# Regrouping batch 0 and batch 1 of a Nystrom attention, gated FFN and soft-MoE kernel: slot tables, paired G products, low bits on ScalarE, three Tanh

## The chip, the cores and the metric

The kernel runs on one core of one Trainium2 chip. The metric is the device time of one execution in microseconds; the median of three runs before the change is 675.02 us (674.23 to 676.28).

## The reference

Three stages follow one another on 8 batches of 576 tokens with 8 heads of 64 (512 features):

```python
q_lm, k_lm = segment means of q, k over 18 tokens       # 32 landmarks per head
A, Bm, C = softmax(q k_lm'), softmax(q_lm k_lm'), softmax(q_lm k')
Z = Bm' / (norm1(Bm) * norminf(Bm));  6 times: Z = 2 Z - Z Bm Z
x = A Z C v                                             # attention, as 4608 x 512
x = (silu(x @ w_gate) * (x @ w_val)) @ w_out            # d_ff = 1536
logits = x @ phi                                        # 32 slots: 8 experts x 4
d = softmax of logits over all 4608 tokens;  c = softmax over the 32 slots
out = c @ expert_ffn(d' x)                              # 8 experts, 512 -> 1024 -> 512
```

## The kernel before

**The loop.** After `first_attention` (attention of batch 0), the main loop runs over batches `b` 0 to 7 and, in each, over twelve chunks `j` of 128 hidden features. `unit(b, j, slot)` does one chunk: for each half of the tokens (288 columns) six matmuls into a PSUM tile `pg` (`mm3`, line 945), an activation on ScalarE (Silu, or Tanh with a multiplication more on VectorE), six matmuls into `pv`, and a product `hT = u * pv` on VectorE (lines 972, 974). There are 288 matmuls of `mm3` in a batch. The weights of these matmuls are `G`, the product of the attention's `WB` with `w_gate` and `w_val` (`g_product`, line 748): ScalarE casts it to `GH` (line 765), VectorE subtracts to get `GL` (`g_low`, line 779). Where `paired(b, j)` holds, one call makes the G of two chunks (512 columns instead of 256).

**The slots.** After each of the four groups of six matmuls `unit` calls `slot(i)`, so that a batch has 48 slots `n = 4 j + i`. Everything else is hung into these slots by the tables in `SCHED`: `u0` (batch 0) and `u` (others) say in which slot of a chunk the next G product, the logits (line 794) and the transposes (line 799) of the chunk before are written; `g_low` follows one slot after the G product. `at1`, `at2`, `at3` list the slots in which the 34 steps of the attention of batch 1, 2 and 3 to 7 are written, one batch ahead: numbers 0 to 7 the landmark sums (line 333), 8 to 11 the scores of A (`m_a`, line 541) and their transposes, 12 to 15 the scores of C (`m_c`) and their copies to `CE` (line 577), 16 to 19 the maxima and exponentials, 22 to 24 the transposes of `CE` (`m_t`, line 631), 26 the product with v, 27 to 32 the six Newton steps (`m_n`, line 672), 33 the new `WB`. Negative numbers are slots of the batch before. `am1` to `am3` do the same for the 17 steps of the softmax of A. `sm1` (batch 1) and `sm` list the ten steps of `softmoe(b - 1)`: copies of the logits, maxima, exponentials (fourth), the transposed exponentials `DN` (fifth, line 867), the spreading of `DN` over partitions (sixth: by twelve DMAs, line 879, and in batch 7 by eight matmuls `m_dr`, line 882), the product `m_d` (seventh, line 913, 144 matmuls), and its addition to `Sacc` (line 923).

**PSUM.** `g`, `m_t`, `m_n`, `m_dr`, and three of the four tiles of `m_a`, `m_c` and `m_d` share the three buffers of the tag `x`; a G product takes two of them until its `GL` is done.

**Batch 0 alone** also converts `w_gate`, `w_val` and `w_out` from 64-bit words (tables `w` and `o`: `f32_top` on ScalarE, line 176, then `f32_bits` on VectorE, lines 192 and 193) and folds `w_out` with phi into `P_sb` (table `p`: `m_wt`, `m_p`, `m_ps`, lines 269, 278, 284).

**What sets the order.** Each engine runs its instructions in the order in which they were issued. From batch 1 on TensorE keeps the order of the program text (`keep_order(mybir.EngineType.PE, middle, ...)`, line 1136, where `middle` is the beginning of batch 1). The order of TensorE in batch 0, and of the other engines throughout, is set by the framework's scheduler, to which the place in the text is a priority. Activations of different tables are fenced by `in_order`. Within a slot the steps run in the order in which the generators were put into `todo`:

```python
    for a in range(1, nb):
        att, asm = attention(a), a_softmax(a)
        for gen, nm in ((att, "at"), (asm, "am")):
            for r in S_[nm + str(min(a, 3))]:
                todo[48 * (a - 1) + r].append(gen)
        sm = softmoe(a - 1)
        for r in S_["sm1" if a == 1 else "sm"]:
            todo[48 * a + r].append(sm)
```

In a slot of batch a the soft-MoE step of batch a - 1 (put in by pass a) thus comes before the attention step of batch a + 1 (put in by pass a + 1).

Of the kernel before, what the change touches and what calls it, by code (L numbers as in the profile page):

```python
# [22 lines left out]
NJ = DFF // 128  # L23
# [31 lines left out]
def nystrom_softmoe_kernel(  # L55
# [681 lines left out]
    def paired(b, j):  # L737
        return 0 < b < nb - 1 and not (b == nb - 2 and j >= NJ - 2)
# [209 lines left out]
    def unit(b, j, slot):  # L948
# [3 lines left out]
        for half in range(2):  # L952
# [3 lines left out]
            by_tanh = 0 < b < nb - 1 and (j, half) in TANH[b > 1]  # L956
# [24 lines left out]
    TANH = [{(5, 0), (5, 1), (6, 0)}, {(1, 1), (2, 0), (2, 1)}]  # L981
# [105 lines left out]
    for a in range(1, nb):  # L1087
        att, asm = attention(a), a_softmax(a)
        for gen, nm in ((att, "at"), (asm, "am")):
            for r in S_[nm + str(min(a, 3))]:  # L1090
                todo[48 * (a - 1) + r].append(gen)
        sm = softmoe(a - 1)
        for r in S_["sm1" if a == 1 else "sm"]:
            todo[48 * a + r].append(sm)
    prev = None
    n_ins = lambda: len(nc.cur_bb.bb.instructions)
    for b in range(nb):
        if b == 1:
            middle = n_ins()
        for j in range(NJ):  # L1100
            p = prev
            def slot(i):
# [27 lines left out]
                if n == (46 if b == 0 else 45) and b + 1 < nb:  # L1130
                    g_unit(b + 1, 0)
                if n == (47 if b == 0 else 46):
                    g_low()
# [211 lines left out]
```

## Time and profile before

| what | value |
|---|---|
| median of the runs | 675.02 us |
| the profiled execution: its time, its span | 674.4 us, 672.6 us |
| busy: TensorE matmul, weight load | 623.9 us (93%), 465.8 us (69%) |
| busy: VectorE, ScalarE, GpSimd | 478.0 us (71%), 298.8 us (44%), 73.3 us (11%) |
| HBM read, written | 91.24 MB, 12.58 MB |

PE is TensorE's matmuls, PEld its weight loads, DVE VectorE, ACT ScalarE, POOL GpSimd, SP SyncE, whose queue (SPq) issues the DMAs. Matmuls are pipelined, and their recorded durations overlap: a busy PE is not PE at its peak. PEclk is the granted share of TensorE's 2.4 GHz. A stretch of this kernel has its own limits, so the batches are read one by one: the first matmul of line 945 starts at 40.4 us, and every 288 of them are a batch, which gives the limits 40.4, 125.9, 200.3, 266.2, 332.1, 398.0, 463.9, 527.7 and 589.8 us for the beginnings of batches 0 to 7 and the end of the last one. Ahead of them lies the attention of batch 0, behind them the expert FFN and the output.

### The profile page before, as it was taken

Reading aid. Unit: us, or ns where it says so; the run is one execution under the profiler, and the core shown is the slowest. Engines: PE = TensorE matmul, PEld = TensorE weight load, DVE = VectorE, ACT = ScalarE, POOL = GpSimd, SP = SyncE. Lnnn points to the kernel's source line nnn. Section 1 sums busy time; section 2 is a strip of 40 time slices with the busy share of each in tenths; the row PEclk is TensorE's granted clock in tenths of the full one; section 3 lists DMA queues with packets and bytes.
Section 4 is the critical chain, followed back from the end, with each engine's and each line's share of the span. In section 5 each row is a group of like instructions: output and inputs, shape, how many; then the busy total and the mean of one; then the engine's idle time right before and its main releaser. Section 6 shows DMA issues by size and latency. Waiting matters only on the chain. (4 is left out here: it accounts for less than half of the span.)

```text
span 672.6 us, 18315 instructions
## 1 busy us (share of the span) xinstructions
PE 623.9 (93%) x7591; PEld 465.8 (69%) x7591; DVE 478.0 (71%) x1154; ACT 298.8 (44%) x764; POOL 73.3 (11%) x81
## 2 busy tenths in 40 slices
PE   5699999998999999999999999999999999989991
PEld 2575667784877877787787778777778777843560
DVE  4999989878578777868785978597856645550441
ACT  2566875445438323732383338233823442320441
POOL 0400012013011101110111012001300000010000
PEclk9799999998999999999999999999999999999996
DMA  8788773233222222222222222122120595699999
GB/s 281 271 322 331 269 280 129 87 113 116 73 72 83 75 72 73 84 75 73 72 86 73 71 87 76 69 71 72 57 86 2 160 378 184 220 288 348 348 369 337
DMA packets 63299, 106.47 MB, mean 158 GB/s; under 512 B 4977, under 2 KB 33009, under 8 KB 61681
## 3 DMA queue, kind: packets, MB, share of 16 engines
q1 hardware_dynamic: 63216, 105.32, 47.1%
q8 instruction: 59, 0.97, 0.6%
q14 instruction: 24, 0.19, 0.1%
HBM read 91.24 MB, written 12.58 MB: 154 GB/s over the span
## 5 line engine op out<-in xcount | busy, mean ns | idle before, releaser
L312 ACT ACTIVATE u<-pg 128x288 f32<-128x288 f32 x174 | 71.9, 413 | 138.4 <-PE pg L945 130.8
L974 DVE TENSOR_TENSOR hT<-u,pv 128x288 f32<-128x288 f32 x174 | 77.7, 447 | 40.1 <-PE pv L945 36.3
L945 PE MATMUL pg<-EH,GH 128*128 128x288 f32 x384 | 93.9, 324 | 2.6 <-ACT GH L765 1.6
L779 DVE TENSOR_TENSOR GL<-g,GH 128x512 fp32r<-128x512 f32 (+1 forms) x122 | 66.4, 572 | 37.7 <-ACT GH L765 37.6
L945 PE MATMUL pg<-EH,GL 128*128 128x288 f32 x384 | 85.7, 299 | 1.7 <-DVE GL L779 1.5
L945 PE MATMUL pv<-EH,GH 128*128 128x288 f32 x384 | 84.0, 298 | 0.0
L945 PE MATMUL pg<-EL,GH 128*128 128x288 f32 x384 | 83.5, 296 | 0.0
L945 PE MATMUL pv<-EL,GH 128*128 128x288 f32 x384 | 82.6, 296 | 0.0
L945 PE MATMUL pv<-EH,GL 128*128 128x288 f32 x384 | 82.2, 295 | 0.0
L765 ACT CAST GH<-g 128x512 fp32r<-128x512 f32 (+1 forms) x122 | 54.2, 495 | 55.0 <-PE g L748 54.9
L945 PEld LDWEIGHTS pg<-EH,GH 128*128 128x128 f32 x384 | 60.0, 189 | 22.8 <-issue 15.5
L799 DVE STREAM_TRANSPOSE HB<-hT 128x576 f32<-128x576 f32 x96 | 74.3, 774 | 1.8
L945 PEld LDWEIGHTS pg<-EH,GL 128*128 128x128 f32 x384 | 62.2, 188 | 4.7 <-DVE GL L779 3.8
L945 PEld LDWEIGHTS pv<-EH,GH 128*128 128x128 f32 x384 | 61.6, 188 | 2.6 <-issue 1.2
L945 PEld LDWEIGHTS pg<-EL,GH 128*128 128x128 f32 x384 | 61.8, 188 | 0.9 <-issue 0.9
L945 PEld LDWEIGHTS pv<-EL,GH 128*128 128x128 f32 x384 | 61.5, 188 | 0.9 <-issue 0.9
L945 PEld LDWEIGHTS pv<-EH,GL 128*128 128x128 f32 x384 | 61.6, 188 | 0.5 <-issue 0.5
L748 PE MATMUL g<-w,WB 64*32 64x512 f32 (+1 forms) x976 | 56.4, 510 | 0.4 <-ACT WB L535 0.4
L794 PE MATMUL l<-hT,P_sb 128*32 128x160 f32 (+1 forms) x768 | 45.2, 298 | 0.8 <-DVE hT L974 0.6
L794 PEld LDWEIGHTS l<-hT,P_sb 128*32 128x32 f32 x768 | 15.2, 108 | 39.8 <-DVE hT L974 16.5
L913 PE MATMUL m_d<-HB,HB 32*32 32x384 f32 x864 | 38.4, 514 | 2.6 <-DMA HB<-DN 2.3
L913 PE MATMUL m_d<-HB,DN 32*32 32x384 f32 x288 | 37.7, 514 | 0.0
(248 smaller groups left out, 946.4 us busy)
## 6 DMA issues: line engine op xcount, KB each, us to landing
k<-in_kT_dram SPq DMA_DIRECT2D x52, 288.0 KB, 3.7
ffn<-in_w_dram SPq DMA_DIRECT2D x13, 1024.0 KB, 9.0
ffn<-in_w_dram SPq DMA_DIRECT2D x24, 512.0 KB, 9.0
HB<-in_w_cat_dram SPq DMA_DIRECT2D x8, 1024.0 KB, 8.0
v<-in_v_dram SPq DMA_DIRECT2D x8, 1024.0 KB, 5.8
q<-in_qT_dram SPq DMA_DIRECT2D x28, 288.0 KB, 3.0
HB<-in_w_out_dram SPq DMA_DIRECT2D x12, 512.0 KB, 5.8
wr<-in_w_cat_dram SPq DMA_DIRECT2D x4, 1024.0 KB, 8.7
```

Source lines behind the costliest of these rows:

```text
L312: i = act.activation(*a, **kw)
L748: pe.matmul(gs[r][32 * hp:32 * hp + 32, 0:256 * n].rearrange("p (u f) -> p u f", u=n), WB[b % 2][64 * r:64 * r + 64, hp, :], w[64 * r:64 * ...
L765: act.copy(H_, g)
L779: dve.tensor_tensor(out=GL, in0=g, in1=GH, op=ALU.subtract)
L794: pe.matmul(L[32 * c:32 * c + 32, 0:32 * k], P_sb[:, j, :], main[:, 0:k, c, :], start=j == 0, stop=j == NJ - 1)
L799: dve.transpose(HB[b % 2][:, S * j:S * j + S].rearrange("p (t r) -> p t r", r=32), hT[:, 0:S].rearrange("p (t r) -> p t r", r=32))
L913: pe.matmul(ms[a][32 * g:32 * g + 32, 0:384].rearrange("p (j f) -> p j f", j=NJ), d_of(a, g, k), hb[32 * a:32 * a + 32, :, 4 * k + g, :], ...
L945: pe.matmul(ps[:, 0:HALF], G_t[b, j, q, sel_][h], e[:, q, ts_], start=n == 0, stop=n == 5)
L974: dve.tensor_tensor(out=o, in0=u, in1=pv[:, 0:HALF], op=ALU.mult)
```

## The change

- **Tables.** All slots of batch 0 change (`w`, `o`, `p`, `at1`, `am1`, `u0`): G, logits and transposes are all written in slot 1 of a chunk, the folding of phi in slots 1 and 3. `at2`, `am2` and `sm1` (attention of batch 2 and soft-MoE of batch 0, both in batch 1) change: `m_a` is written in slot 5 instead of 9, `m_c` in 13 instead of 17, the transposes of `CE` in 17 instead of 23, two slots after the last copy instead of four; the spreading of `DN` in slot 18 instead of 21, `m_d` in slot 25 instead of 24. A new table `sm7` (soft-MoE of batch 6, in batch 7) has `DN` in slot 10 and its spreading in slot 13, where `sm` has both in slot 7.
- **Loads.** `v1` is loaded last of the first loads; `w3` moves ahead of `w4`. The k of batch 2 is loaded in slot 36 (`lq`) instead of 44.
- **Low bits.** For the chunks 2, 3, 5, 7, 9 and 11 of `w`, ScalarE makes the low bits (one activation over 1024 elements) and VectorE one instruction per 512 columns instead of two.
- **G pairs** also in batch 0, from chunk 4 on; the G of batch 1's chunk 0 is written in slot 45 instead of 46.
- **Tanh** in three halves of batch 0; the three of batch 1 move by four slots.
- **The order in a slot.** The soft-MoE steps are put into `todo` in a loop of their own, after all attention steps.

```diff
-    'w': [[-22, 2], [-12, 2], [0, 3], [1, 3], [6, 3], [10, 3], [14, 3], [18, 3], [20, 4], [28, 4], [24, 4], [33, 4]],
-    'o': [[-6, 1], [3, 2], [5, 3], [9, 3], [13, 3], [17, 3], [21, 3], [25, 3], [29, 3], [33, 3], [37, 3], [41, 3]],
-    'p': [[0, 2, 2], [5, 2, 1], [10, 2, 1], [14, 2, 1], [18, 2, 1], [22, 2, 1], [26, 2, 1], [30, 2, 1], [34, 2, 1], [38, 2, 1], [42, 2, 1], [46, 1, 0]],
-    'loads': ['w1', 'q0', 'o0', 'w0', 'v0', 'o1', 'q1', 'v1', 'w2', 'w4', 'p', 'w3'],
-    'at1': [1, 2, 3, 3, 4, 5, 6, 6, 7, 7, 8, 8, 9, 9, 10, 10, 12, 13, 13, 13, 16, 17, 18, 19, 20, 21, 22, 26, 28, 31, 34, 37, 40, 43],
-    'am1': [20, 21, 22, 22, 24, 24, 26, 27, 28, 30, 32, 34, 36, 37, 39, 41, 42],
-    'at2': [-3, -2, -1, 0, 3, 4, 5, 6, 9, 10, 10, 11, 17, 18, 18, 19, 19, 20, 20, 21, 21, 22, 23, 23, 23, 25, 27, 29, 31, 33, 35, 37, 39, 42],
-    'am2': [12, 12, 13, 13, 20, 21, 22, 23, 24, 25, 27, 29, 31, 32, 34, 36, 37],
+    'w': [[-22, 2], [-12, 2], [0, 3], [4, 3], [6, 4], [8, 4], [12, 4], [15, 4], [19, 4], [23, 4], [27, 4], [31, 4]],
+    'o': [[-6, 1], [1, 2], [4, 3], [8, 3], [12, 3], [16, 3], [20, 3], [24, 3], [28, 3], [32, 3], [36, 3], [40, 3]],
+    'p': [[-1, 2, 2], [3, 2, 2], [7, 2, 2], [11, 2, 2], [15, 2, 2], [19, 2, 2], [23, 2, 2], [27, 2, 2], [31, 2, 2], [35, 2, 2], [39, 2, 2], [43, 2, 2]],
+    'loads': ['w1', 'q0', 'o0', 'w0', 'v0', 'o1', 'q1', 'w2', 'w3', 'w4', 'p', 'v1'],
+    'at1': [0, 1, 2, 3, 4, 5, 6, 6, 7, 8, 9, 10, 11, 12, 15, 16, 16, 17, 17, 18, 18, 19, 19, 19, 21, 22, 23, 27, 29, 33, 35, 37, 39, 43],
+    'am1': [11, 12, 13, 13, 18, 18, 20, 22, 23, 24, 25, 28, 30, 31, 32, 33, 36],
+    'at2': [-3, -2, -1, 0, 3, 4, 5, 5, 5, 6, 6, 7, 13, 14, 14, 15, 15, 16, 16, 17, 17, 17, 17, 17, 17, 19, 21, 25, 27, 29, 31, 33, 37, 41],
+    'am2': [7, 8, 8, 9, 16, 17, 18, 19, 19, 20, 22, 23, 25, 26, 27, 28, 30],
     'sm': [1, 2, 3, 6, 7, 7, 25, 26, 26, 28],
-    'sm1': [1, 2, 4, 19, 20, 21, 24, 25, 25, 28],
+    'sm1': [1, 2, 4, 15, 17, 18, 25, 26, 26, 28],
+    'sm7': [1, 2, 3, 6, 10, 13, 25, 26, 26, 28],
-    'u0': [1, 3, 3, 0],
+    'u0': [1, 1, 1, 0],
-    'lw': [0, 0, 0, 0, 0, 0, 0, 0, 0, 0, 0, 0],
+    'lw': [0, 0, 1, 1, 0, 1, 0, 1, 0, 1, 0, 1],
-    'lq': 44,
+    'lq': 36,
...
     def paired(b, j):
-        return 0 < b < nb - 1 and not (b == nb - 2 and j >= NJ - 2)
+        return (b > 0 or j >= 4) and b < nb - 1 and not (b == nb - 2 and j >= NJ - 2)
...
-            by_tanh = 0 < b < nb - 1 and (j, half) in TANH[b > 1]
+            by_tanh = b < nb - 1 and (j, half) in TANH[min(b, 2)]
...
-    TANH = [{(5, 0), (5, 1), (6, 0)}, {(1, 1), (2, 0), (2, 1)}]
+    TANH = [{(4, 1), (5, 0), (5, 1)}, {(4, 0), (4, 1), (5, 0)}, {(1, 1), (2, 0), (2, 1)}]
...
                 todo[48 * (a - 1) + r].append(gen)
+    for a in range(1, nb):
         sm = softmoe(a - 1)
-        for r in S_["sm1" if a == 1 else "sm"]:
+        for r in S_["sm1" if a == 1 else "sm7" if a == nb - 1 else "sm"]:
             todo[48 * a + r].append(sm)
...
-                if n == (46 if b == 0 else 45) and b + 1 < nb:
+                if n == 45 and b + 1 < nb:
                     g_unit(b + 1, 0)
-                if n == (47 if b == 0 else 46):
+                if n == 46:
                     g_low()
```

## Rows read from the trace of the kernel before

**Rows 1.** Engines by stretch (start:end, length, busy us and count): batches 0, 1, 3.

```profile
40.40:125.90 85.50, 81.74 (x931) 60.00 (x930) 78.73 (x182) 59.88 (x141) 8.75 (x7) 1.00 0.72 262
125.90:200.30 74.40, 70.83 (x863) 53.23 (x860) 54.91 (x131) 31.50 (x82) 10.59 (x10) 0.98 0.28 86
266.20:332.10 65.90, 64.79 (x827) 51.00 (x826) 51.77 (x127) 29.06 (x77) 8.45 (x8) 1.00 0.25 77
```

**Rows 2.** Line 945 alone in the same stretches: PE busy, PEld busy, clock.

```profile
40.40:125.90 85.50, 50.84 (x288) 40.00 (x288) 1.00 0.72 262
125.90:200.30 74.40, 43.46 (x289) 39.03 (x290) 0.98 0.28 86
266.20:332.10 65.90, 41.83 (x291) 38.75 (x290) 1.00 0.25 77
```

**Rows 3.** Timeline of VectorE in batch 0: start, length, instruction.

```profile
45.93 0.72 DVE L192 TENSOR_SCALAR w<-w 128x512 int32<-128x512 int32 x2
46.56 1.29 DVE L193 SCALAR_TENSOR_TENSOR w<-HB,w 128x512 int32<-128x512 int32 x2
```

**Rows 4.** VectorE groups of batch 0: instructions, busy us, mean ns, idle before.

```profile
L974 DVE TENSOR_TENSOR hT<-u,pv 128x288 f32<-128x288 f32 x24 | 10.7, 447 | 2.2 <-PE pv L945 1.7 <-ACT u L312 0.6
...
L779 DVE TENSOR_TENSOR GL<-g,GH 128x256 fp32r<-128x256 f32 x24 | 9.2, 416 | 0.5 <-ACT GH L765 0.5
```

**Rows 5.** ScalarE groups of batch 0.

```profile
L312 ACT ACT_TABLE_LOAD x5 | 6.4, 1283 | 0.9 <-DVE stat L608 0.9
L176 ACT ACTIVATE w<-HB 128x1024 f32<-128x1024 f32 x6 | 6.9, 1147 | 0.0
```

**Rows 6.** The product m_d alone: batches 1 and 3.

```profile
125.90:200.30 74.40, 7.96 (x144) 3.98 (x144) 0.00 (x0) 1.70 (x4) 0.98 0.28 86
...
266.20:332.10 65.90, 4.32 (x144) 2.52 (x144) 2.35 (x4) 0.00 (x0) 1.00 0.25 77
```

**Rows 7.** Timeline of batch 1: the spreading of DN by DMA, and m_d.

```profile
152.77 7.81 SPq L879 DMA_DIRECT2D HB<-DN  x12
...
161.87 0.51 PE L913 MATMUL m_d<-HB,HB 32*32 32x384 f32 x2 [2.28 <-DMA HB<-DN]
```

**Rows 8.** Engines in five us around that m_d; the clock is third from the end.

```profile
160.00:165.00 5.00, 3.13 (x91) 1.99 (x99) 5.00 (x11) 1.34 (x2) 2.86 (x2) 0.79 0.30 77
```

**Rows 9.** Timeline of batch 1: a paired G product, its casts, the next matmuls, GL.

```profile
131.86 1.09 PE L748 MATMUL g<-w,WB 64*32 64x512 f32 x16
...
133.04 1.07 ACT L765 CAST GH<-g 128x512 fp32r<-128x512 f32 x2 [1.46 <-PE g L748]
133.28 0.53 PE L945 MATMUL pg<-EH,GH 128*128 128x288 f32 x2
...
133.66 1.29 DVE L779 TENSOR_TENSOR GL<-g,GH 128x512 fp32r<-128x512 f32 x2 [1.17 <-ACT GH L765]
```

**Rows 10.** Timeline of batch 1: the second transposes of CE.

```profile
155.44 0.63 PE L631 MATMUL m_t<-cst,CE 128*128 128x128 f32 x4 [0.20 <-ACT CE L312]
```

**Rows 11.** Timeline of batch 3, slot 25: m_d, Sacc, the Newton step, the next matmuls.

```profile
299.56 0.51 PE L913 MATMUL m_d<-HB,DN 32*32 32x384 f32 x1
...
303.86 1.14 DVE L923 SCALAR_TENSOR_TENSOR Sacc<-Sacc,al,m_d 128x384 f32<-128x384 f32 x2 [4.07 <-PE m_d L913]
304.53 0.69 PE L672 MATMUL m_n<-RV,bd 128*128 128x96 f32 x4 [0.65 <-DVE Sacc L923]
305.00 0.51 PE L945 MATMUL pg<-EH,GH 128*128 128x288 f32 x2
...
306.18 0.28 DVE L688 TENSOR_TENSOR RV<-RV,m_n 128x128 f32<-128x128 f32 x1
```

**Rows 12.** Timeline of batch 7, slot 7: the matmuls before, m_dr, the matmuls after.

```profile
536.19 0.42 PE L945 MATMUL pv<-EH,GL 128*128 128x288 f32 x2
...
538.53 0.55 PE L882 MATMUL m_dr<-DN,cst 32*128 32x160 f32 x6 [1.92 <-DVE DN L867]
...
539.94 0.54 PE L945 MATMUL pg<-EH,GH 128*128 128x288 f32 x2
```

## The prediction

> **What bounds the kernel now.** I read the busy times batch by batch, not over the whole span. Batches 2 to 5 take 65.9 us each; there TensorE is idle for 1.1 us and VectorE for 14, so the order of TensorE's work is the bound [rows 1]. Batch 0 takes 85.5 and batch 1 74.4 us for the same 288 matmuls of line 945. In batch 0 VectorE is busy for 78.73 of 85.5 us, nearly all of it, and TensorE looks full too (81.74). But line 945 alone is busy for 50.84 us there against 41.83 in batch 3 [rows 2]: 9.0 us are matmuls that wait behind one another or start anew after other work has cut in. So batch 0 hangs on VectorE's queue and on how often TensorE's work is cut up; batch 1 has a few waits of TensorE in a fixed order. Those are what the change can reach; batches 2 to 6 keep their tables, and only the order within a slot changes there.
>
> **Batch 0.** First VectorE's work. *Low bits:* in six chunks two shifts of 512 columns go away; two of them advance VectorE by 46.56 - 45.93 = 0.63 us [rows 3], so 6 x 0.63 = 3.8 us. The merging instruction stays; that it is as long with the other operands is assumed, the row being the same form. *Pairs:* four times, four subtractions of 256 columns (416 ns [rows 4]) become two of 512, for which a pair in batch 1 shows 1.29 us [rows 9]: 4 x (1.66 - 1.29) = 1.5 us less. *Tanh:* three multiplications more; no such row in batch 0, so the nearest, a two-input product of the same 288 columns, 447 ns [rows 4]: 1.3 us more. Net 4.0 us less, 78.73 becomes 74.7. TensorE's need, taken from batch 3's way of running: 85.5 less the 9.0 us of line 945 and less the idle time above batch 3's (3.8 - 1.1 = 2.7) is 73.8 us. So neither engine lets batch 0 go below some 75 us: at most 10.8 us are there. The least is nothing, if the waits stay where the scheduler puts them. I take 60 in 100 of the way, 6.5 us (batch 0 in 79.0), nearer to the upper end, because the steps of one slot now lie side by side, and the exponentials lie in two neighbouring slots with Tanh around them, so that of five table loads of 1283 ns [rows 5] about two should go (2.6 us of ScalarE).
>
> The price is paid by ScalarE: the low bits have no row; the nearest is the activation over the same 1024 elements, 1147 ns [rows 5], 6.9 us in all, so 59.88 becomes about 64 of 79 us (81%) with the table loads off. I take it as hidden; without that cover it costs the difference to VectorE's time, 6 x (1.15 - 0.63) = 3.1 us, and the VectorE gain besides.
>
> The Trainium skill speaks against this edit: "ScalarE: Activation LUTs", section "Rules for kernel authors", would have adds and multiplies on VectorE and not on ScalarE. By that rule the term would be plus 3.1 us instead of minus 3.8; the trace agrees with the rule on the single instruction (1147 ns against 630 for the two), but here VectorE is the fuller engine.
>
> The loads change order only: `v1` is wanted late (slot 23), the words of `w` earlier. I cost that at nothing; it is covered by the conversions, which are now four slots apart. Bounds: one to two us either way. On SP's queue the k of batch 2 is issued eight slots earlier, behind the same loads; nothing waits for it there.
>
> **Batch 1.** Three things to gain. `m_d` is busy for 7.96 us against 4.32 [rows 6] and sat idle for 2.28 more, because the twelve DMAs were issued from 152.77 us on and landed at 161.87 [rows 7]: 3.6 + 2.3 = 5.9 us. In the thin stretch the granted clock fell: 0.79 over 160 to 165 us [rows 8], part of it at 1.2 GHz, and line 945 is busy for 43.46 instead of 41.83 us [rows 2]: 1.6 us. `m_d` now stands seven slots behind the spreading instead of three; a slot is 65.9 / 48 = 1.37 us, so 9.6 us against the 9.1 that the DMAs took. So 7.5 us go, if no new hole takes the clock down.
>
> But TensorE's order is fixed here, and four steps get into each other's way. *Slots 5 and 13* now hold a paired G product ahead of `m_a` and of `m_c`. A G product holds two of the three `x` buffers until GL is done, 133.66 + 1.29 = 134.95 us, while TensorE was free to go on at 133.28 [rows 9]. `m_a` and `m_c` want three; the first half can use the free one, the second waits: 1.3 us each (0 to 1.7), and the chunk's next matmuls are queued behind it. *Slot 17* has the transposes of CE two slots behind the last copy instead of four. In the old order TensorE already waited 0.20 us for the exponential [rows 10]. Two slots of 41.83 / 48 = 0.87 us and a G product of 1.09 that lay between are gone, two casts of 1.07 us on ScalarE too [rows 9]: 0.2 + 1.74 + 1.09 - 1.07 = 2.0 us (0 to 3). *Slot 25* see next, 0.7. Together 5.3; batch 1 gains 7.5 - 5.3 = 2.2 us (from 7.5 faster to 2 slower).
>
> **Batches 2 to 6.** With the soft-MoE steps put in after the attention steps, slot 25 has the Newton step ahead of `m_d`, where it came after. Now: `m_d` starts at 299.56, the Newton step waits 0.65 us for Sacc, the next chunk starts at 305.00: 5.44 us [rows 11]. Then: the Newton step takes one `x` buffer and gives it back when RV is done, which took from 304.53 to 306.46, 1.9 us; `m_d` needs all three and so starts in full 1.9 us later, and takes 303.86 - 299.56 = 4.3: 6.2 us in all. The Sacc addition lay in that 1.9, so I take a little less than the difference: 0.7 us more per batch, 3.5 in five batches (bounds: 0.65 less each if a buffer is free after all, 0.8 more each with nothing in VectorE's way). The exponentials of slots 6 and 7 change places; nothing there ends a wait of TensorE, so nothing.
>
> **Batch 7.** `m_dr` waits for DN: from 536.61 to 539.94 us, 3.3 us, TensorE gets nothing done but eight small matmuls [rows 12]. Three slots between DN and `m_dr` cover that wait of 1.92. But slot 13 also has a G product, with two of three buffers. Of the 3.3 I leave 1.7: 1.6 us gained (0 to 2.3).
>
> **The sum.** The profiled execution took 674.4 us (span 672.6). 674.4 - 6.5 - 2.2 + 3.5 - 1.6 = 667.6. The median of the runs is 0.6 above that execution, so 668.2 us. What follows batch 7 moves with it.
>
> **The rivals.**
> - *All the way:* both engines of batch 0 get to 75.8 (9.7 us less), and no `x` buffer is short: batch 1 then gains 7.5 - 2.0 = 5.5, batches 2 to 6 nothing. 674.4 - 9.7 - 5.5 - 1.6 + 0.6 = 658.2. For it: idle time of VectorE in batch 0 is small already. Against: three buffers are three.
> - *It doesn't do what it says:* the scheduler cuts TensorE's work in batch 0 as before and the spared VectorE time goes into other waits: 674.4 - 2.2 + 3.5 - 1.6 + 0.6 = 674.7.
> - *ScalarE becomes the bound of batch 0,* the casts and Silu queue behind the low bits: 3.1 us more there, 677.8. Against: it has 21 us of room. This is the mechanism by which the rule named above would be right.
> - *Slower, by the Newton step ahead of `m_d` in six batches:* if its three evictions stand in VectorE's queue behind a GL pair (1.29) [rows 9] and a Sacc pair (1.14) [rows 11], each costs up to 3.1 us instead of 0.7. The other terms gain 11.0, so from 1.8 us a batch on the change is slower than before; at 2.6 it gives 679.6. Against: in slot 25 of batch 3 VectorE was idle for 4.07 us [rows 11].
>
> **Chances and range.** 0.3% (2.0 us) is about what a measurement of this kernel can tell from no change. Forecast (664 to 672) 0.50; all the way 0.14; not as it says 0.15; ScalarE 0.06; slower 0.15. Faster: 0.50 + 0.14 and a little of the third, 0.65; same: the rest of it, half of ScalarE's and some of the last, 0.19; slower 0.16. From 658 to 679 all but the ends of the first and last rival lie inside.
>
> **What would show it.** Batch 0 near 79 us with line 945 at about 46 busy, VectorE near 75. In batch 1 no DMA wait of `m_d`, the clock at 1.0, and instead waits of `m_a`, `m_c` for GL and of `m_t` for CE. In batches 2 to 6 66.6 us each, with `m_n` ahead of `m_d`. In batch 7 no wait for DN. Batches of 65.9 or less would refute the buffer argument, a batch 0 above 84 the VectorE argument.

## The result, and the profile after the change

The changed kernel takes 679.55 us (678.91 to 680.83), the kernel before 676.28 us in the same comparison: 1.006 times as long, interval 1.0041 to 1.0078 (this ratio, like the later ones, is the one on record; the quotient of the two medians is 1.0048). The profiled executions are 680.83 and 674.4 us. New lines shift the numbers a little: the product of line 945 is now line 946, `m_d` line 914, `m_wt` line 270, `m_n` line 673.

Where the 6.4 us between the two profiled executions lie (each batch from its first matmul of line 946 to the next batch's, batch 7 to the end of its last matmul of that line, which in the kernel before is 588.4 us and not the 589.8 given ahead of the prediction; the tail from there to the end of the span):

| us | batch 0 | 1 | 2 to 5, each | 6 | 7 | tail |
|---|---|---|---|---|---|---|
| before | 85.5 | 74.4 | 65.9 | 63.9 | 60.7 | 84.2 |
| after | 85.7 | 76.0 | 66.3 | 64.6 | 59.2 | 88.0 |
| difference | +0.2 | +1.6 | +0.4 | +0.7 | -1.5 | +3.8 |

Engines by stretch of the changed kernel, batches 0, 1 and 3, columns as in [rows 1]:

```profile
40.20:125.90 85.70, 79.85 (x866) 61.11 (x865) 73.98 (x164) 61.60 (x137) 8.86 (x7) 0.94 0.66 227
125.90:202.00 76.10, 70.35 (x860) 52.52 (x859) 53.73 (x131) 31.34 (x81) 10.58 (x10) 0.98 0.27 82
334.60:400.90 66.30, 65.67 (x827) 51.12 (x826) 51.29 (x127) 29.38 (x77) 8.30 (x8) 1.00 0.25 77
```

Line 946 alone in the same stretches, as in [rows 2], and `m_d` alone in batches 1 and 3, as in [rows 6]:

```profile
40.20:125.90 85.70, 48.62 (x288) 40.32 (x289) 0.94 0.66 227
125.90:202.00 76.10, 42.47 (x290) 38.96 (x290) 0.98 0.27 82
334.60:400.90 66.30, 41.84 (x291) 38.69 (x290) 1.00 0.25 77
```

```profile
125.90:202.00 76.10, 6.53 (x144) 3.25 (x144) 0.00 (x0) 1.72 (x4) 0.98 0.27 82
334.60:400.90 66.30, 5.12 (x144) 2.61 (x144) 2.19 (x4) 0.00 (x0) 1.00 0.25 77
```

ScalarE groups of batch 0, as in [rows 5]: three table loads instead of five, and the new low bits.

```profile
L313 ACT ACT_TABLE_LOAD x3 | 3.8, 1283 | 0.1
L184 ACT ACTIVATE wr<-wr 128x1024 int32<-128x1024 uint16 x3 | 3.7, 1225 | 0.0
L184 ACT ACTIVATE HB<-HB 128x1024 int32<-128x1024 uint16 x3 | 3.5, 1161 | 0.0
```

VectorE has 4.75 us less to do in batch 0 than in [rows 1], and the batch is no shorter. Two things stand in it instead. First a stop of TensorE; its timeline in batch 0 of the changed kernel (start, length, instruction, in brackets the idle time and what ended it):

```profile
54.50 0.41 ACT L313 ACTIVATE u<-pg 128x288 f32<-128x288 f32 x1 [1.64 <-PE pg L946]
54.81 1.12 ACT L177 ACTIVATE w<-wr 128x1024 f32<-128x1024 f32 x1
54.83 0.42 PE L946 MATMUL pv<-EH,GL 128*128 128x288 f32 x2
...
55.81 1.12 ACT L184 ACTIVATE wr<-wr 128x1024 int32<-128x1024 uint16 x1
56.82 1.21 ACT L177 ACTIVATE HB<-HB 128x512 f32<-128x512 f32 x2
...
58.17 0.42 DVE L193 TENSOR_SCALAR HB<-HB 128x512 int32<-128x512 int32 x1
58.63 0.69 DVE L194 SCALAR_TENSOR_TENSOR HB<-HB 128x512 int32<-128x512 int32 x1
...
59.38 0.90 PE L270 MATMUL m_wt<-cst,HB 128*128 128x128 f32 x3 [4.12 <-DVE HB L194]
```

`m_wt` of chunk 2 waits for the conversion of w_out's chunk 2, which queues on ScalarE behind the top and the low bits of w's chunk 5. Then the clock: windows of the same kernel behind that stop, the granted clock third from the end.

```profile
55.00:60.00 5.00, 0.88 (x5) 0.65 (x5) 4.20 (x8) 3.03 (x4) 0.00 (x0) 0.91 0.00 0
60.00:65.00 5.00, 5.00 (x47) 2.05 (x45) 3.13 (x8) 3.24 (x6) 0.00 (x0) 0.50 0.95 344
65.00:70.00 5.00, 5.00 (x45) 2.85 (x45) 3.68 (x7) 1.01 (x3) 1.85 (x2) 0.57 1.00 372
```

TensorE is idle for 4.1 of the five us, and then runs at 1.2 GHz until 69 us.

In batch 1 the DMA wait of `m_d` [rows 7] is gone; these waits of TensorE (us in total, times, longest) are there instead:

```profile
PE m_t L632 <- ACT CE L313: 1.8, 2, 1.0
PE l L795 <- DVE hT L975: 1.0, 1, 1.0
PE m_d L914 <- ACT RV L680: 0.7, 1, 0.7
PE l L795 <- DVE hT L973: 0.6, 1, 0.6
...
PE m_a L542 <- DVE GL L780: 0.4, 1, 0.4
PE m_c L542 <- DVE GL L780: 0.3, 1, 0.3
```

Slot 25 of a later batch, the answer to [rows 11]: the Newton step first, four matmuls of `m_d` into the free buffer, and the rest when VectorE has done with the step's buffer:

```profile
367.98 0.69 PE L673 MATMUL m_n<-RV,bd 128*128 128x96 f32 x4
...
368.94 0.48 PE L914 MATMUL m_d<-HB,HB 32*32 32x384 f32 x1
369.52 0.29 DVE L689 TENSOR_TENSOR RV<-RV,m_n 128x128 f32<-128x128 f32 x1 [0.33 <-ACT RV L688]
369.86 0.52 PE L914 MATMUL m_d<-HB,HB 32*32 32x384 f32 x3 [0.44 <-DVE RV L689]
```

In batch 7 `m_dr` follows without the wait of [rows 12]: from 547.58 to 549.61, 2.0 us where 3.3 passed.

```profile
547.58 2.10 PE L883 MATMUL m_dr<-DN,cst 32*128 32x160 f32 x8
549.61 0.54 PE L946 MATMUL pg<-EH,GH 128*128 128x288 f32 x2
```

And in the tail there is a stop that the kernel before does not have, inside the last `m_d`, for no reason that the profile shows ("issue"):

```profile
599.83 0.53 PE L914 MATMUL m_d<-HB,HB 32*32 32x384 f32 x4
...
602.08 0.48 PE L914 MATMUL m_d<-HB,DN 32*32 32x384 f32 x1 [1.72 <-issue]
```

With the stop this `m_d` takes 8.0 us from its first matmul to its last where 5.5 passed, 2.5 of the tail's 3.8 us. The other 1.3 come behind it; what they are was not separated.

### The profile page after: what moved, and what is told of

It is laid out like the page before. It is cut to its first block, busy times and chain, and to the rows that moved or that the text cites. A ratio compares the mean times of both kernels' runs of the same rounds, so it can differ in the third digit from the quotient of the medians.

```text
span 679.0 us, 18167 instructions
## 1 busy us (share of the span) xinstructions
PE 627.9 (92%) x7527; PEld 468.5 (69%) x7527; DVE 469.2 (69%) x1137; ACT 302.9 (45%) x760; POOL 72.8 (11%) x81
## 5 line engine op out<-in xcount | busy, mean ns | idle before, releaser
L313 ACT ACTIVATE u<-pg 128x288 f32<-128x288 f32 x171 | 70.5, 413 | 166.4 <-PE pg L946 154.8
L780 DVE TENSOR_TENSOR GL<-g,GH 128x512 fp32r<-128x512 f32 (+1 forms) x114 | 64.9, 599 | 36.8 <-ACT GH L766 36.6
L946 PE MATMUL pv<-EH,GH 128*128 128x288 f32 x384 | 83.8, 296 | 0.0
L766 ACT CAST GH<-g 128x512 fp32r<-128x512 f32 (+1 forms) x114 | 53.6, 522 | 55.6 <-PE g L749 55.4
L914 PE MATMUL m_d<-HB,HB 32*32 32x384 f32 x864 | 42.5, 512 | 2.9 <-DVE RV L689 2.2
L914 PE MATMUL m_d<-HB,DN 32*32 32x384 f32 x288 | 40.8, 512 | 1.7 <-issue 1.7
```

The costliest lines, as they stand in the source:

```text
L313: i = act.activation(*a, **kw)
L766: act.copy(H_, g)
L780: dve.tensor_tensor(out=GL, in0=g, in1=GH, op=ALU.subtract)
L914: pe.matmul(ms[a][32 * g:32 * g + 32, 0:384].rearrange("p (j f) -> p j f", j=NJ), d_of(a, g, k), hb[32 * a:32 * a + 32, :, 4 * k + g, :], ...
L946: pe.matmul(ps[:, 0:HALF], G_t[b, j, q, sel_][h], e[:, q, ts_], start=n == 0, stop=n == 5)
```

## The experiments

Eighteen kernels, each with its profile; "us" is the median of its runs, "ratio" that to the kernel before on the same chip (674.6 to 676.3 us), the rest the stages of the one profiled execution. In e1, e4, e10 and e15 that execution is the longest and 3.2 to 4.3 us above the median, so that a stage of theirs can lie above the usual one. "Stop" is TensorE's stop inside the last `m_d`, "records" the matmul records of TensorE in the whole trace. They are named by their first numbers (e1 is e1_low_on_vector).

| kernel | us | ratio (interval) | batch 0 | 1 | 3 | 7 | tail | stop | records |
|---|---|---|---|---|---|---|---|---|---|
| before | | 1 | 85.5 | 74.4 | 65.9 | 60.7 | 84.2 | none | 7591 |
| after | 679.55 | 1.006 (1.0041 to 1.0078) | 85.7 | 76.0 | 66.3 | 59.2 | 88.0 | 1.72 | 7527 |
| e1 | 683.43 | 1.0106 (1.0066 to 1.0145) | 89.6 | 77.2 | 66.3 | 59.2 | 87.7 | 1.84 | 7527 |
| e2 | 681.14 | 1.0094 (1.0073 to 1.0115) | 87.7 | 73.9 | 66.3 | 60.7 | 88.7 | 2.09 | 7527 |
| e3 | 675.62 | 1.0013 (0.9997 to 1.0028) | 85.2 | 73.4 | 65.9 | 60.8 | 87.2 | 1.83 | 7527 |
| e4 | 674.78 | 1.0003 (0.9987 to 1.0019) | 85.8 | 70.0 | 66.3 | 60.7 | 89.4 | 2.19 | 7527 |
| e5 | 672.94 | 0.9961 (0.9945 to 0.9978) | 85.8 | 70.3 | 65.9 | 59.2 | 87.8 | 1.74 | 7527 |
| e6 | 679.6 | 1.0061 (1.0038 to 1.0084) | 88.4 | 74.6 | 66.3 | 60.7 | 84.4 | none | 7555 |
| e7 | 678.36 | 1.004 (1.0022 to 1.0057) | 87.8 | 74.0 | 66.3 | 60.7 | 83.6 | none | 7591 |
| e8 | 680.0 | 1.0064 (1.0034 to 1.0093) | 86.1 | 76.6 | 66.3 | 59.2 | 86.6 | 1.67 | 7527 |
| e9 | 671.91 | 0.9945 (0.9925 to 0.9966) | 86.0 | 69.6 | 65.9 | 59.4 | 86.9 | 1.34 | 7527 |
| e10 | 672.99 | 0.9969 (0.9955 to 0.9982) | 85.7 | 70.2 | 65.9 | 60.7 | 90.1 | 2.26 | 7527 |
| e11 | 675.3 | 1.0013 (0.9989 to 1.0037) | 87.6 | 70.2 | 65.9 | 59.2 | 85.0 | none | 7555 |
| e12 | 670.75 | 0.9938 (0.9917 to 0.996) | 84.2 | 69.9 | 65.9 | 59.5 | 85.9 | 1.49 | 7527 |
| e13 | 669.16 | 0.9925 (0.9906 to 0.9944) | 84.9 | 70.5 | 65.9 | 59.2 | 83.8 | none | 7559 |
| e14 | 668.37 | 0.9911 (0.9891 to 0.993) | 83.0 | 70.0 | 65.9 | 59.6 | 86.7 | 1.54 | 7527 |
| e15 | 670.0 | 0.9935 (0.9918 to 0.9952) | 84.6 | 70.5 | 65.9 | 60.7 | 87.8 | 2.30 | 7527 |
| e16 | 672.51 | 0.9964 (0.9949 to 0.9978) | 85.4 | 70.7 | 65.9 | 60.7 | 87.1 | 1.47 | 7527 |
| e17 | 676.94 | 1.0021 (1.0003 to 1.0039) | 91.3 | 69.8 | 65.9 | 60.7 | 84.1 | none | 7559 |
| e18 | 672.62 | 0.9974 (0.9954 to 0.9995) | 89.3 | 69.4 | 65.9 | 59.2 | 84.2 | none | 7559 |

### Is the stop ahead of m_wt what holds batch 0? (e1, e2, e6, e8)

e1: low bits back on VectorE.

```diff
-    'lw': [0, 0, 1, 1, 0, 1, 0, 1, 0, 1, 0, 1],
+    'lw': [0, 0, 0, 0, 0, 0, 0, 0, 0, 0, 0, 0],
```

> The changed kernel with the low bits of all chunks back on VectorE (lw all 0). In its trace TensorE stands still from 55.2 to 59.4 us behind ScalarE's conversions of chunk 5 (top 1.12, low bits 1.12 us) and of w_out's chunk 2, and the granted clock is 0.5 for the 10 us behind it; batch 0 takes 85.7 us. Theory A (the hole comes from where m_wt of chunk 2 stands, three slots behind the conversion that feeds it): with the low bits taken out of ScalarE's queue the hole shrinks by no more than 1.1 us, the clock falls all the same, VectorE has 3.8 us more to do: batch 0 86 to 88, total 680 to 683. Theory B (the low bits on ScalarE are what stops TensorE): hole below 2 us, clock 1.0 throughout, batch 0 79 to 81, total 673 to 676.

The stop stays (4.3 us) and the clock is at 0.5 for longer, so theory B falls. Batch 0 takes 89.6, more than either theory gave: 3.9 us more than with the low bits on ScalarE, beside the 3.8 of the sum. The match is not clean: the half clock lasts 17.1 us instead of 10.2, which can be up to 3.4 us of it.

e2: the folding of w_out later.

```diff
-    'p': [[-1, 2, 2], [3, 2, 2], [7, 2, 2], [11, 2, 2], ...
+    'p': [[-1, 2, 2], [3, 2, 2], [9, 2, 1], [13, 2, 1], ...
```

> The changed kernel with the folding of w_out (m_wt, m_p, m_ps) from chunk 2 on written two slots later, so that it stands five slots behind its conversion, as in the kernel before; low bits stay on ScalarE. Theory A (place of m_wt): no stop of TensorE above 2 us between 50 and 70 us, granted clock 1.0 there, so the hole (4.1 us) and the half clock (10.2 us at half speed, some 4 to 5 us) both go: batch 0 76 to 79 us, total 670 to 673. Theory B (low bits on ScalarE): the wait only moves on to a later place in the chain of conversions, batch 0 83 to 86, total 677 to 680. Rival C (the clock falls for another reason than the stop): hole gone, clock 0.5 still there: batch 0 81 to 82, total 675.

The stop at 55 us is gone, but ten us later the first paired G waits for its GL behind VectorE's conversions, and the clock falls there (timeline line, then windows of e2):

```profile
68.95 0.51 PE L946 MATMUL pg<-EH,GL 128*128 128x288 f32 x1 [2.38 <-DVE GL L780]
```

```profile
65.00:70.00 5.00, 2.62 (x27) 1.67 (x23) 5.00 (x9) 1.35 (x3) 1.11 (x1) 0.91 0.99 380
70.00:75.00 5.00, 5.00 (x57) 3.58 (x54) 3.06 (x11) 3.79 (x8) 0.00 (x0) 0.50 0.98 392
```

The first four chunks take 25.4 us instead of 35.0, the other eight 62.3 instead of 50.8: batch 0 is longer. Theory A was right on the stop and wrong on the batch.

e6: the stop filled with work.

```diff
             mm3(pv, b, j, 1, half)
+            if (b, j, half) == (0, 2, 1):
+                for _ in range(14):
+                    pe.matmul(pv[:, 288:448], ident, cst[:, 128:288], start=True, stop=True)
```

> The changed kernel with 14 extra matmuls of 160 columns behind the last product of batch 0's chunk 2, into unused columns of its PSUM tile, so that TensorE works through the 4.1 us in which it waits for m_wt; nothing that it waits for comes earlier. Theory A (the clock falls because TensorE stood still): granted clock 1.0 between 55 and 72 us, batch 0 4 to 6 us shorter (80 to 82), total 674 to 676. Rival (the clock falls for another reason): clock 0.5 for 7 to 10 us there again, batch 0 85 to 87, total 679 to 681. A second question goes with it: in five traces of changed kernels TensorE stands still for 1.7 to 2.2 us inside the last m_d of the program, always between its 135th and 141st of 144 matmul records, beside a transfer of 16 KB of its instructions. If that is the place where a new piece of code begins, the 28 records more ahead of it move the stop to about the 110th; if it hangs on the data of m_d, it stays at the 138th.

Windows of e6 at the place of the stop and around chunk 6:

```profile
55.00:60.00 5.00, 5.00 (x38) 4.77 (x36) 2.01 (x4) 3.60 (x5) 0.00 (x0) 1.00 0.00 0
60.00:65.00 5.00, 4.12 (x62) 1.56 (x61) 3.95 (x9) 2.06 (x5) 0.00 (x0) 1.00 0.78 274
85.00:90.00 5.00, 2.97 (x22) 1.47 (x21) 5.00 (x11) 3.69 (x8) 1.11 (x1) 0.77 0.26 62
90.00:95.00 5.00, 5.00 (x42) 4.72 (x45) 4.28 (x12) 3.08 (x7) 0.00 (x0) 0.54 0.91 350
```

With TensorE at work through 55 to 60 us the clock stays at 1.0: so far theory A holds. It gives back less than was expected, for the first four chunks take 32.8 us instead of 35.0: 2.2 us, where half of the 10.2 us of half clock would be 5.1. And a stop of 2.0 us comes at 86 us, the clock falls behind that one, and batch 0 takes 88.4, the other eight chunks 55.6 of them.

e8: w_out's chunk 2 first on ScalarE.

```diff
+            with tc.issue_after(fence['o2']) if (kind, j) == ('w', 5) else nullcontext():
                 todo_[i]()
```

> The changed kernel with one order added on ScalarE: both activations of w's chunk 5 (top 1.12, low bits 1.12 us) behind the top of w_out's chunk 2, which m_wt waits for. Theory (the hole is this queue order on ScalarE and not a lack of time): m_wt of chunk 2 starts 1.5 to 2.3 us earlier, the stop is 1.8 to 2.6 us instead of 4.1, the half clock behind it is shorter or gone: batch 0 78 to 83 us, total 673 to 677. Rival (chunk 5 is then late by the same amount and the wait moves to the G product of chunks 4 and 5): batch 0 85 to 87, total 679 to 681.

The stop is 2.47 us, within what was expected, so it is that queue order. The clock still falls, from 61 to 72 us, and batch 0 takes 86.1: in time its rival held. In all four the stop or its half clock changed, and the batch did not get shorter. In e2 and e6 the time came back in the other eight chunks; in e8 the first four did not get shorter (35.4 us).

### Which step of the change costs what in batches 1 to 6? (e3, e4, e5)

e3: within a slot the soft-MoE step first again (the second loop over `a` taken out).

```diff
-    for a in range(1, nb):
         sm = softmoe(a - 1)
```

> The changed kernel with one thing undone: within a slot the soft-MoE step of batch a-1 again comes ahead of the attention step of batch a+1 (so in slot 25 m_d ahead of the first Newton step). Theory A (the Newton step holds an x buffer and its evictions hold up m_d): batches 2 to 6 go from 66.3 back to 65.9 us, in batch 1 the 0.7 us wait of m_d for RV goes: 2.5 to 3.5 us less, total 676 to 677. Rival (order within the slot is worth nothing, the 0.4 us come from elsewhere, the Tanh or the pairing state that batch 1 leaves): batches 2 to 6 stay at 66.3, total 679 to 680.

Batches 2 to 5 are back at 65.9 us, batch 1 at 73.4. Theory A. In batch 1 2.6 us go, more than the 0.7 of the one wait; what the rest of them is was not separated.

e4: in batch 1 only the soft-MoE table stays changed (`at2`, `am2` and `TANH[1]` as before).

> The changed kernel with batch 1's attention tables at2, am2 and its Tanh halves as they were before; only the soft-MoE table of batch 1 stays changed (spreading of DN in slot 18 instead of 21, seven slots ahead of m_d). Theory A (batch 1 loses its gain by m_a, m_c and m_t standing too close behind G products and casts): no DMA wait of m_d, and the waits of m_t for CE (1.8 us) and of m_a, m_c for GL (3.0 us) go: batch 1 from 76.0 to 71 to 73 us, total 675 to 677. Rival (m_d and the granted clock are what batch 1 loses by, wherever the attention stands): clock 0.5 in some stretch again, batch 1 74.5 or more, total 678 to 680.

Batch 1 in e4 (columns as above):

```profile
126.50:196.60 70.10, 67.75 (x860) 51.49 (x859) 54.88 (x131) 33.46 (x83) 10.57 (x10) 1.00 0.27 89
```

70.0 us at clock 1.00, with no wait above 0.5 us (the longest is a stop inside `m_d`, see below): the early spreading alone gains 4.4 us on the kernel before, and the regrouped attention steps cost 6.0.

e5: both undoings.

> The two single undoings together: the changed kernel with soft-MoE steps ahead of attention steps within a slot, and with at2, am2 and the Tanh halves of batch 1 as before; the early spreading of DN in batch 1 and the whole of batch 0 stay changed. If the two are separate terms, batch 1 takes 69 to 70 us and batches 2 to 6 65.9 each (63.9 the sixth): total 671 to 673. Rival (both undoings give back the same time, because both relieve the x buffers around slot 25): total 674 to 675.5.

672.9 us, faster than the kernel before by 0.4%; its profiled execution is the median one. In batch 1 the two are one term (70.3 against 70.0: with the old table the Newton step does not stand in slot 25), in batches 2 to 6 the order is one of its own.

### What in batch 0 costs, what pays? (e7, e9, e10, e12, e16)

e7: no pairs in batch 0.

```diff
-        return (b > 0 or j >= 4) and b < nb - 1 and ...
+        return b > 0 and b < nb - 1 and ...
```

> The changed kernel with the four paired G products of batch 0 undone (chunks 4 to 11 again one by one), all else as changed. The pairs' term of the sum was minus 1.5 us of VectorE: if it counts in full, batch 0 is 1.5 us longer (87.2); if the hole and the half clock at 55 to 70 us set batch 0 before the first pair comes, and the rest hangs on VectorE, between 86 and 88; if pairs cost by holding x buffers, batch 0 84 to 85. With 64 matmul records more ahead of the last m_d, as in the kernel before, the stop of 1.7 us inside it goes (theory: place in the code) or moves to its 74th record; rival (DMA traffic alone): it stays near the 138th. Total 677 to 681.

Batch 0 is 2.1 us longer; the pairs' term was 1.5.

e9, e10 and e12 stand on e5. e9 takes back the tables `w` (chunks 0 to 7), `o`, `p`, `loads` and `u0`; e10 takes back `at1` and `am1`; e12 both, so that in batch 0 little but low bits, pairs and Tanh stays of the change (chunks 8 to 11 of `w`, which the pairs need earlier, stay too, and `lq`).

> The kernel with both undoings (soft-MoE steps first, batch 1's tables as before; batch 0 there takes 85.8 us, 672.9 in all), and in batch 0 the conversion of the weights put back where it was: tables w (chunks 0 to 7), o, p, the order of the loads and the slots of G, logits and transposes as before the change. Low bits on ScalarE, the pairs, the Tanh halves and the earlier attention of batch 1 stay changed. In the changed kernel the first four chunks of batch 0 take 35.0 us against 26.7 before, the other eight 50.7 against 58.8. Theory A (the two groups per chunk, with m_wt close behind its conversion, cost the first four chunks their 8 us): first four chunks 27 to 29 us, batch 0 77 to 80, total 665 to 668. Rival (the low bits on ScalarE, or the attention of batch 1 that now comes earlier, slow the first chunks): first four chunks 33 to 36 again, batch 0 84 to 87, total 671 to 674.

> The kernel with both undoings (672.9 us, batch 0 85.8), and the attention steps of batch 1 (at1, am1) put back into the slots that they had before; the regrouped conversion of batch 0 stays. Theory A (the regrouped conversion is what costs): the stop of 4.1 us ahead of m_wt and the half clock behind it stay, batch 0 84 to 88, total 671 to 675. Rival (the earlier attention steps cost the first four chunks their 8 us): batch 0 77 to 80, total 664 to 668.

> The kernel with both undoings, and in batch 0 every table as before the change; only the three parts that the sum of the prediction counted stay: low bits of six chunks on ScalarE (minus 3.8 us of VectorE), four G pairs (minus 1.5) and three Tanh halves (plus 1.3). Theory A (these parts pay and the regrouping cost): batch 0 79 to 82 us, total 666 to 669. Rival (batch 0 is set by a chain of conversion, G and PSUM buffers in which the spared VectorE time lies idle): batch 0 84 to 86, VectorE below 75 us busy, total 671 to 673.

In e9 the first four chunks take 25.7 us instead of 35.1, better than expected; the other eight take 60.3 instead of 50.7. Theory A was right on the chunks and wrong on the batch (86.0). e10 stays at 85.7, with the stop of 4.1 us as expected, but only 3.4 us of half clock behind it. e12 gives 84.2, 1.3 us less than before: its rival holds, except that VectorE is 75.75 busy.

e16 (e12 with `TANH[0]` empty):

> The kernel e12_parts_alone with Silu in all halves of batch 0, so without the three Tanh halves (VectorE 1.1 us less by the trace of the changed kernel). If the Tanh halves cost what their multiplications take: batch 0 83 us, total 669.5. If they save table loads (e12_parts_alone still has five): batch 0 85 to 87, total 671.5 to 673.

85.4 us, 1.2 more than with Tanh. It is not the table loads (five in both), and in e16 the clock was at 0.5 for 3.4 us from 99 us on, which can cost up to 1.7 us by itself: inconclusive.

### What sets batch 0, then? (e14, e15, e17, e18)

e14 and e15 take work out of e12.

```diff
+        if n == 1024:
+            return [lambda: None] * (4 if low_by_act else 5)
```

> The kernel e12_parts_alone without the merging of low bits into the gate and value weights, on VectorE and on ScalarE (the weights come out 2 to the power of 112 too small, so the output is not the reference's). VectorE has 15 us less to do in batch 0 (ten chunks of 1.3 to 2.1 us), ScalarE 6.9 less. Theory A (VectorE's queue sets batch 0, so that what it is spared comes out): batch 0 72 to 77 us. Rival B (TensorE's order and the shared PSUM buffers set it): batch 0 80 to 84, VectorE idle for 20 us and more. Total follows: 659 to 664 against 667 to 671.

> The kernel e12_parts_alone without the ScalarE activation that extracts the low bits of six chunks; VectorE's merge is as long, but merges nothing (the output is not the reference's). ScalarE has 6.9 us less to do, VectorE the same. Theory C (ScalarE's queue sets batch 0): batch 0 78 to 80 us, total 664 to 667. Rival (ScalarE has room, as the prediction took it): batch 0 83 to 85, total 669 to 671.

Batch 0 in e12, then in e14:

```profile
40.50:124.70 84.20, 78.54 (x868) 59.07 (x867) 75.75 (x167) 65.37 (x139) 8.69 (x7) 1.00 0.75 267
```

```profile
39.40:122.30 82.90, 78.38 (x867) 58.87 (x866) 61.59 (x139) 59.13 (x133) 8.51 (x7) 1.00 0.75 272
```

14.2 us less on VectorE and 6.2 less on ScalarE shorten the batch by 1.2 us; TensorE's busy time does not change. ScalarE's low bits alone (e15) are worth nothing (84.6). With the tables of before, which e12 and its kin have, VectorE's queue thus does not set batch 0, nor does ScalarE's. In both traces no wait of TensorE ends with a DMA, and the waits of the other engines that do come to 1.1 and 1.7 us. What is left is TensorE's own work and its order; that these set the batch is an inference by elimination.

e17 and e18 (on e13, below) hold TensorE to the order of the text in batch 0, e17 with the tables of before, e18 with the regrouped ones.

```diff
-        if b == 1:
+        if b == 0:
             middle = n_ins()
```

> The kernel e13_unpaired_late (669.2 us, batch 0 84.9, line 946 there in 43 runs) with TensorE held to the order of the text from batch 0 on instead of batch 1; the tables of batch 0 are those of before, so that its matmuls stand in 48 runs of six, with one to three other steps between. Theory D (each cut costs some 0.2 us, and that is most of what batch 0 has above 75): five runs more, 1 us longer, 85 to 87, total 669 to 671. Rival E (the scheduler's order is there to avoid waits; fixed, TensorE waits for conversions and casts): 88 to 95 us with waits of m_wt, m_p and g of 1 us and more, total 672 to 680.

> The same fixed order with the regrouped tables of batch 0 (as changed, also at1 and am1): 24 runs of twelve matmuls with the other steps in two groups per chunk. Theory D (cuts): 12 to 19 runs fewer than with the scheduler's order, 2 to 4 us shorter: batch 0 80 to 83 us, no long stop ahead of m_wt of chunk 2 (its place in the text has four groups of other work ahead of it), total 664 to 668. Rival E (waits): TensorE stands still for G, m_wt or m_p in each group, batch 0 86 to 95, total 671 to 680.

Both are longer (91.3 and 89.3 us), and rival E holds; in e17 3.6 of TensorE's 11.1 idle us are one wait for the load of phi. In e18 line 946 stands in 24 runs (43 in e13, 36 in the changed kernel), and TensorE waits:

```profile
PE m_wt L270 <- DVE HB L194: 3.5, 1, 3.5
PE m_ps L285 <- ACT HB L280: 3.1, 1, 3.1
PE m_t L632 <- ACT P_sb L286: 1.6, 1, 1.6
PE m_n L673 <- ACT HB L280: 1.5, 2, 0.8
```

The waits of that view are 11.1 us in all, which leaves 78.2. Three stretches of 3.4 us at half clock cost at most half of their length, 5.1 more: 89.3 - 16.2 = 73.1. So TensorE's need in few runs is, by this estimate, between 73.1 and 78.2 us. The 73.8 of the prediction can be right, but it is not shown, and no order that was tried has few runs and no waits.

### The stop in the last m_d (e6, e7, e11, e13)

The 13 kernels with 7527 records stop, always behind the 135th to the 139th of the 144 records of that `m_d`, for 1.34 to 2.30 us. The seven with another count (28, 32 or 64 more) do not. Their tails are 85.9 to 90.1 and 83.6 to 85.0 us. In the stretch of the stop code is being fetched on q8 beside the weights of the FFN (queues of the changed kernel, 599 to 604 us):

```profile
q1 hardware_dynamic: 1014, 1.02, 58.1%
q8 instruction: 2, 0.03, 2.9%
```

e11 (on e5) adds 14 small matmuls at the end of the first attention, e13 (on e12) undoes two pairs in batch 6:

```diff
-        ... and not (b == nb - 2 and j >= NJ - 2)
+        ... and not (b == nb - 2 and j >= NJ - 6)
```

> The kernel with both undoings (672.9 us) and 14 small extra matmuls (32 columns, into unused columns) at the end of the first attention, ahead of batch 0; nothing else is changed. They move all later work of TensorE by 28 records further on in its code. Theory (the stop of 1.7 to 2.2 us in the last m_d is where new code has to come while the loads of the FFN fill the DMA queues): no stop there, from the end of the last product of line 946 to the end 84 to 85 us instead of 87.8, total 670 to 671.5. Rival (the stop comes from the data or the DMA traffic of that moment): stop at the 136th to 138th record again, total 672.5 to 673.5.

> The kernel e12_parts_alone (670.75 us) with two G pairs of batch 6 (chunks 6 to 9) undone, which gives TensorE 32 records more ahead of the last m_d; VectorE has some 14 idle us in that batch, so the batch itself should stay at 63.8 to 64.2 us. Theory (where a piece of TensorE's code ends decides on the stop in the last m_d): no stop above 0.5 us there, from the last product of line 946 to the end 83.5 to 85 us instead of 85.9, total 668.5 to 670. Rival (data or DMA traffic of that moment): stop of 1.5 us at the 134th record again, total 670.5 to 671.5.

In both the stop is gone and the tail shorter by 2.8 and 2.1 us, as expected; that it would move to the 110th record, as e6's expectation had it, was wrong. In e11 batch 0 begins 3.0 us later than in e5 and takes 1.8 us longer, so its total misses (675.3). In e13 batch 6 costs 0.9 us more than in e12, which was not expected, and the total is 669.2 us: by its median the fastest kernel here that leaves nothing out, 0.75% below the kernel before (e12's interval overlaps with its own). Its last `m_d` ends and goes straight on:

```profile
592.37 0.50 PE L914 MATMUL m_d<-HB,HB 32*32 32x384 f32 x2
592.80 1.68 PE L808 MATMUL warm<-cst 128*128 128x160 f32 x8
```

When the pieces of code land says more. In all 13 kernels that stop, one piece of 16 KB on q8 begins to move during this `m_d`, and TensorE goes on 1.2 to 1.5 us after its transfer has ended (in the changed kernel the transfer lasts from 599.90 to 600.86 us, and the next matmul starts at 602.08). A transfer alone does not do it: e6, e11 and e17 have one during this `m_d` too and do not stop. Nor does it take full DMA queues. In six kernels (e4, e5, e9, e10, e12, e15) the `m_d` of batch 1 stops in the same way, behind its 131st to 134th record, for 0.3 to 1.0 us, again 1.2 to 1.5 us after a piece has landed; in e12 the DMA engines are 3% busy there (timeline line, then the window around it, the DMA share last but one):

```profile
161.86 0.52 PE L914 MATMUL m_d<-HB,HB 32*32 32x384 f32 x4 [0.94 <-issue]
```

```profile
159.50:162.00 2.50, 1.56 (x71) 0.72 (x46) 2.50 (x7) 0.67 (x1) 0.75 (x2) 1.00 0.03 8
```

The Trainium skill ("Runtime: NRT & Kernel Launch", section "Instruction fetch mechanics") has the code refilled in blocks of 256 instructions and crossing into the next one mostly hidden. The traces agree on the blocks: q8 moves 59 pieces of 16 KB in the whole changed kernel, by that figure 15104 instructions (an estimate), and TensorE has 2 x 7527 = 15054 records. Hidden the crossing was not at these two places. That the stop is a late block is the reading that fits all twenty traces; that the fetch was waited for is not itself in a row, and why e13, e14 and e16 do not stop in batch 1 is open.

## Why the prediction was wrong

**Batch 0 (minus 6.5, came +0.2): the step that failed** is "batch 0 hangs on VectorE's queue", with the 60 in 100 taken from it. The work went as summed: VectorE 78.73 to 73.98 (74.7 forecast), low bits 1.16 and 1.23 us an activation (1.15 taken), two table loads fewer. But a busy share of 92% was taken for a bound. e14 shows the price of that, with the tables of before: of 14.2 us taken from VectorE, 1.2 came out. With the tables of the change so much was never left out.

The other half of the step, TensorE's work cut up less often, came in part. Before, TensorE is busy for 81.74 us at clock 1.00. After, it is busy for 79.85 us at clock 0.94, so (1 - 0.94) x 85.7 = 5.1 us of that are the half clock if it costs half of its length, and 2.2 by e6: 74.7 to 77.6 us at full clock (an estimate), where the prediction had 73.8. What took this gain away are two terms that the prediction put at nothing in batch 0: 2.1 us more of idle time (5.85 against 3.76), most of it the stop ahead of `m_wt`, and the 2.2 to 5.1 us of half clock behind it. But easing them did not shorten the batch (e6, e8), so this sum tells where the time lies and not what sets it. Whatever was eased, the batch stayed between 83 and 91 us, as the rival "it doesn't do what it says" had it (spared time goes into other waits). Which order would bring TensorE to some 74 us stays open.

The rule of the Trainium skill that the prediction weighed ("ScalarE: Activation LUTs", section "Rules for kernel authors") would have made the low bits cost 3.1 us. No run shows that: ScalarE's activations left out are worth nothing (e15), and in the changed order taking the low bits back cost 3.9 us, though up to 3.4 of them by a longer half clock (e1).

**Batch 1 (minus 2.2, came +1.6).** The mechanisms were there: no DMA wait, and instead `m_t` 1.8 us (2.0 forecast) and the waits for GL. Their price by e4 was 6.0 us for 5.3, but that they are so near is in part luck: the waits of `m_a` and `m_c` for GL came to 0.7 us instead of 2.6, and the sum had neither the 1.6 us in which the logits wait for `hT` nor a half clock of 3.4 us at 168 us (up to 1.7). Mis-sized was the gain: 4.4 us instead of 7.5. The 1.6 us laid to the clock were not there: line 946 takes 43.32 us in batch 1 of e5 too, at clock 1.00 (43.46 in [rows 2]).

**Batches 2 to 6 (+0.7 each, came +0.4, the sixth +0.7)** went by the step named, the Newton step holding a buffer: e3 took it back to 65.9. The rival "slower by the Newton step" came near the total, 679.6, but for 0.4 us a batch and not 2.6: a right number by a wrong reason.

**Batch 7 (minus 1.6, came minus 1.5)** was right. In nine of the nineteen kernels with `sm7` the gain is missing from the profiled execution (60.7 us): the wait for DN is gone there too, but the clock is at 0.5 for 3.4 us in that batch.

**The tail (to move with batch 7, came +3.8): the second step that failed.** Nothing in the profile of before showed that four pairs, 64 records fewer, would make TensorE stop in the last `m_d`. Without the tail's 3.8 us, of which that `m_d` has 2.5, the two profiled executions would differ by 2.6.

## What to carry to other kernels

A busy share near one does not make an engine the bound: before counting its spared time as time, name who waits for it, and if possible take far more of its work away than the change does, and see what comes out. A stop that is removed shows its worth only in the length of its stage, for it may come back a few us later. And where one change bundles several, take each part back alone: here two of them cost 4 to 5 us each and 6.6 together by the medians (e3, e4, e5), and hid that the rest is 0.4% faster than the kernel before (e5), and 0.75% in the best selection (e13).

## What the runs showed of the hardware

- Inside a burst of 144 small matmuls TensorE stopped for 1.3 to 2.3 us, at the same place in the 13 kernels with the same count of records and in none of the seven with another. It went on 1.2 to 1.5 us after a 16 KB piece of code had landed. Shorter stops of that kind (0.3 to 1.0 us) came in batch 1 of six kernels, with the DMA engines 3% busy in e12. No wait in the profile names it; the row says "issue".
- After stops of TensorE of 2.0 to 4.3 us in batch 0 the granted clock was at 0.5 for 3.4 to 17 us. After stops of 1.35 to 1.75 us it fell in e9, e15, e16 and e18 and stayed at 1.0 in e12 and e13; e12 and e16 have the same stop of 1.7 us at 98 us. In batch 7 it fell in nine kernels without any stop above 0.12 us, and 3.4 us at half clock cost 1.5 us there (60.7 against 59.2). A stop in the last `m_d` was followed by it in some kernels and not in others (windows of e4, where it was):

```profile
600.00:605.00 5.00, 4.59 (x18) 2.54 (x18) 2.51 (x7) 0.33 (x1) 2.62 (x3) 0.50 0.68 180
605.00:610.00 5.00, 4.67 (x24) 0.99 (x24) 0.92 (x6) 0.00 (x0) 0.00 (x0) 0.54 0.95 312
```
